# A fused attention and gMLP kernel: VectorE's exponential becomes one fourth power plus a linear term

## The chip, the core and the metric

The kernel runs on one core of a Trainium2 chip. The metric is the device time of one execution in microseconds; lower is better. The time before is the median of three runs.

## The reference

Two branches read the same input x (1 x 2048 x 512, bfloat16) and are mixed by a sigmoid gate per row. Branch A is attention with 32 heads of 16 channels that share one key and one value head. Branch B is a gMLP with a spatial matrix of 2048 x 2048.

```python
g = _sigmoid((x * gate_w).sum(-1, keepdims=True))
# A: H = 32, Dh = 16, one K and one V for all heads
q = (x @ wq).reshape(B, S, H, Dh).transpose(0, 2, 1, 3)
k = x @ wk
v = x @ wv
p = _softmax(jnp.einsum('bhqd,bkd->bhqk', q, k) * Dh ** (-0.5), axis=-1)
a = jnp.einsum('bhqk,bkd->bhqd', p, v).transpose(...).reshape(B, S, H * Dh) @ wo
# B: Fh = 688
z = _gelu(jnp.einsum('bsd,df->bsf', x, w_in))
z1 = z[..., :Fh]; z2 = _layernorm(z[..., Fh:])
gg = jnp.einsum('ts,bsf->btf', w_sp, z2) + b_sp[None, :, None]
b = jnp.einsum('bsf,fd->bsd', z1 * gg, w_out)
out = g * a + (1 - g) * b
```

## The kernel before

**Blocks.** The scores of all heads are 32 x 2048 x 2048 numbers. The kernel cuts them into 32 units. A unit is four heads and 512 queries, and within it there are 16 key tiles of 128 keys for each of the four heads (called groups, g). One block is 128 keys by 512 queries of one head, so a unit has 64 blocks and the kernel 2048. TensorE (PE) computes a block with a 32-row matmul (`s_mm`) into one of the eight PSUM banks; four such matmuls, one for each group, can run side by side. The exponential of a block is a 128 x 512 tile in SBUF, and a second matmul (`o_mm`) multiplies it by the 128 x 32 tile of V (with a column of ones for the softmax's sum) and adds it up in bank 6, four groups side by side again. Four matmuls side by side are called a round here.

**Two ways to an exponential.** ScalarE (ACT) reads two or three banks with one `Exp` and writes bfloat16 into a ring of `PB` = 16 tiles called P (`exp_op`, line 827). VectorE (DVE) makes a part of the blocks by a polynomial in float16. A batch is one key tile of a unit, four blocks (2048 columns). For a batch, `d_A` (line 839) reads the score s from PSUM and writes Q_A * s + Q_AS into a buffer U; `d_u` (line 846) squares U in place; `d_w` (line 852) squares once more, out of place, into a buffer W. The exponential is approximated, up to a common factor, by W's fourth power, the second power in U with a weight, a linear term and a constant. So each block has two products with V: U meets V1, and W meets VW, a copy of V scaled by Q_CW that GpSimd (POOL) makes at the start (line 570). The linear and the constant term need no elementwise work: per unit they are one matmul each with sums over the keys that are formed once (KTV and SVB). There are `ND` = 5 pairs of U and W.

`d_w` is shared: VectorE or POOL does it, in pieces of 256 columns, eight to a batch. POOL works upward from the end of a batch and VectorE from its start.

**The gMLP and the rest.** PE's other work comes in small pieces that fill the time between the blocks: the projections, z1 and z2 (win times x), the spatial product (`g_sp`), the outputs (`g_out`). After z1 and z2 are there, at some 160 us, ACT breaks off its exponentials for one stretch of GELU (`gelu_ops`, line 653), with a change of its function table on either side. VectorE then takes the statistics of z2 (line 659), POOL raises the variance to the power of -0.5 (line 668), and VectorE normalises z2 (line 673).

**The planner.** The order of all instructions on all engines is fixed before the kernel runs, by a planner written in Python in the same file: it plays through the run with estimated durations for PE, ACT, VectorE and POOL (`pe_step`, `act_step`, `dve_step`, `pool_step`) and issues, at each step, what its rules choose. Semaphores follow from the reads and writes of tiles (`Prog.op`). Its rules have numbers that were chosen by hand or search, in `PR`. These matter here:

- VectorE has two banks of its own, `DBK` = (5, 4). The second is shared with ACT's three-bank steps; `FLEX` says up to which backlog of VectorE it goes to VectorE instead.
- `D_HG` is the backlog of VectorE below which PE refills its banks right after a score step.
- POOL starts a piece of `d_w` only where VectorE's next work reads PSUM for long enough (`psum_work`, `pool_try`), since the planner takes VectorE's SBUF squares and POOL's to exclude each other (`lock`).
- `WRES` is the reserve of pieces that VectorE leaves to POOL when it is not urgent; pieces of the unit that PE is adding up come first (`poly_step`).
- `NXT` and `RMIN` bound how far VectorE works ahead into the next unit and how late in a unit a batch may start.
- When PE has nothing, it runs filling matmuls with zeros as long as its busy share over the last 3400 ns is under `W_MIN`.

A batch's buffer is free again when all its products with V have been issued (`dleft`). A flag computed on the chip compares the largest |q|^2 |k|^2 with 0.985 * Q_B^2; where it is exceeded, all of attention is computed again in a general way.

Of the kernel before, what the change touches and what calls it, by code (L numbers as in the profile page):

```python
# [7 lines left out]
ALU = mybir.AluOpType  # L8
# [7 lines left out]
D = 512  # L16
# [7 lines left out]
PB = 16  # L24
ND = 5
NQ = 3
NMAX = 8
NXT = 32
Q_B = 0.74
Q_A = 0.4770697274170593  # L30
Q_AS = 0.5048945666981567
Q_C0 = 0.6939921791513274
Q_C1 = 0.32473621688265525
Q_CW = 0.78515625
# [13 lines left out]
A_OV = 63.7  # L48
# [5 lines left out]
C_P0 = 184.0  # L54
C_WT = 4500.0
# [5 lines left out]
PR = dict(HALF=50.0, IDR=10, IDN=4, WRES=20, D_HG=2400.0, D_FL=False, WIN=1000.0, WIH=560.0, BACK=30, PRESS=5, FLEX=3000.0, RMIN=32, WBL=0.4, W_MIN=0.85, TTR=0.0, PMX=3, WMX=1000.0, PTO=6000.0, PSL=80.0, WP0=45000.0, WG=0, HOLD=0.0, RLEND=0)  # L61
# [109 lines left out]
def build_kernel(nc, x_d, wq_d, wk_d, wv_d, wo_d, win_d, wsp_d, bsp_d, wout_d, gw_d, out_d):  # L171
    es = ExitStack()
    with es:
# [13 lines left out]
        def bkey(b):  # L187
            return ("bk", b)
# [11 lines left out]
        VW = sb("VW", [128, NMAX, 32], B16)  # L200
# [6 lines left out]
        UW = sb("UW", [128, 2, ND, 2048], F16)  # L207
# [35 lines left out]
        wq_raw = UW[:, 1, ND - 1, :].bitcast(B16).rearrange("p (a n) -> p a n", a=4)  # L243
# [297 lines left out]
        def g_V(c, b=BM):  # L541
            nw = 2 * DH + 1
            kn = 4 * c + 4 > NKT - NMAX

            def piece(k, dt):
                t0 = 512 * c + 128 * k
                return lambda: fm(b, nw, 64 * k, xT[:, dt, t0:t0 + 128], wvg[:, dt, 0:nw], dt == 0, dt == 3, ["wv", "gw", "wvk", ("x", c)], "V")
            src = bank(b, 256).rearrange("p (k w) -> p k w", w=64)
            evs = []

            def e1():
                op("dve", lambda v: v.tensor_copy(V1[:, 4 * c:4 * c + 4, 0:DH], src[:, :, 0:DH]), r=[bkey(b)], w=[("V", c)], tag="Vev")

            def e2():
                op("dve", lambda v: v.tensor_scalar(gs[:, 4 * c:4 * c + 4].unsqueeze(2), src[:, :, 2 * DH:2 * DH + 1], E_MAX, None, ALU.min), r=[bkey(b)], w=[("gs", c)], tag="gsev")

            def e3(e):
                k0 = 4 * c - (NKT - NMAX)
                return lambda: op("dve", lambda v: v.tensor_scalar(KN[:, k0:k0 + 4, e, 16 * e:16 * e + 16], src[:, :, DH:2 * DH], 0.25, None, ALU.mult),  # L559
                                  r=[bkey(b)], w=["KN"], tag="KNev")  # L560
            evs = [(150.0, e1), (100.0, e2)]
            if kn:
                evs += [(140.0, e3(0)), (140.0, e3(1))]

            def done(t):
                T[("V", c)] = t
                if kn:
                    k0 = 4 * c - (NKT - NMAX)
                    fin = kn and all(("V", c2) in T for c2 in (2, 3))
                    dq(pl_q, 600.0, lambda: op("pool", lambda g: g.tensor_scalar(VW[:, k0:k0 + 4, :], V1[:, 4 * c:4 * c + 4, :], Q_CW, None, ALU.mult),  # L570
                                               r=[("V", c)], w=["VW"], tag="VW"), t, setT("VW") if fin else None)
# [77 lines left out]
        def gelu_ops():  # L649
            out = []  # L650
            for k in range(4):
                def f(k=k):
                    op("act", lambda a: a.activation(z2[:, 4 * k * FH:4 * (k + 1) * FH], z2[:, 4 * k * FH:4 * (k + 1) * FH], ACT.Gelu_apprx_tanh),  # L653
                       r=[("z2", 4 * k + i) for i in range(4)], w=[("z2", 4 * k + i) for i in range(4)], tag="gelu2")
                    t = clk["now"] + 2600.0
# [9 lines left out]
                    if k == 3:  # L665
                        def pw():
                            op("dve", lambda v: v.tensor_scalar(ve[:], mv[:, :, 1], LN_EPS, None, ALU.add), r=[("mv", i) for i in range(NST)], w=["ve"])
                            op("pool", lambda g: g.tensor_tensor(rstd[:], ve[:], nhalf[:], ALU.pow), r=["ve", "nhalf"], w=["rstd"])
                            t2 = clk["now"] + 4500.0
                            zc = [NST]  # L670
                            for st in range(NST):
                                def zn(st=st):
                                    op("pool" if st in ZP else "dve", lambda v: v.tensor_scalar(z2[:, FH * st:FH * st + FH], z2[:, FH * st:FH * st + FH], mv[:, st, 0:1],  # L673
                                                                        rstd[:, st:st + 1], ALU.subtract, ALU.mult),
                                       r=[("mv", st), "rstd", ("z2", st)], w=[("z2", st)], tag="z2n")
                                    zc[0] -= 1
                                    if not zc[0]:
                                        T["z2n"] = clk["now"] + (C_ZN if st in ZP else 370.0) + 200.0
                                if st in ZP:
                                    dq(pl_q, C_ZN, zn, t2, None)  # L680
                                else:
                                    dq(dve_q, 370.0, zn, t2, "tt")
                        dq(dve_q, 220.0, pw, t)
                out.append((2490.0, f, []))
            for ft in range((NZ - ZD) // 4):
                def f(ft=ft):
                    op("act", lambda a: a.activation(z1[:, ft, :], z1[:, ft, :], ACT.Gelu_apprx_tanh), r=[("z1", ft)], w=[("z1", ft)], tag="gelu1")
                    T[("gelu", ft)] = clk["now"] + 2000.0
                out.append((1905.0, f, [("z1", ft, tc) for tc in range(4)]))
# [147 lines left out]
        def d_A(m, i, b, n=1):  # L837
            s = m % ND
            op("dve", lambda v: v.tensor_scalar(UW[:, 0, s, 512 * i:512 * (i + n)], bank(b, 512 * n), Q_A, Q_AS, ALU.mult, ALU.add),  # L839
               r=[bkey(b + j) for j in range(n)], w=[("U", s, h) for h in range(i, i + n)], tag="dA")  # L840

        def d_u(m, h0, h1):
            s = m % ND
            src = UW[:, 0, s, 1024 * h0:1024 * h1]
            k = [("U", s, h) for h in range(2 * h0, 2 * h1)]
            op("dve", lambda v: v.tensor_tensor(src, src, src, ALU.mult), r=k, w=k, tag="dTT")  # L846

        def d_w(eng, m, a, b, after=()):
            s = m % ND
            src = UW[:, 0, s, 256 * a:256 * b]  # L850
            w = [("W", s, i) for i in range(a, b)] + (["wqr0", "wqr1"] if s == ND - 1 else [])
            op(eng, lambda v: v.tensor_tensor(UW[:, 1, s, 256 * a:256 * b], src, src, ALU.mult),  # L852
               r=[("U", s, h) for h in range(a // 2, (b + 1) // 2)], w=w, after=after, tag="dTT" if eng == "dve" else "pTT")
# [146 lines left out]
        gst = {"on": False, "arm": False, "t": 0.0}  # L1000
# [51 lines left out]
        def new_batch(now):  # L1052
# [6 lines left out]
            for u in (ua, ua + 1):  # L1059
# [24 lines left out]
                dleft[m] = 8  # L1084
# [448 lines left out]
        def act_step(now):  # L1533
# [12 lines left out]
            if gst["arm"] and (gel or dz["i"] < NZ or dz["cur"] is not None or dz["full"]) and st_["ke"] == st_["kf"] or gst["on"]:  # L1546
                r = None
                extra = 0.0 if gst["on"] else 1300.0
# [45 lines left out]
        def uw_add(m, z, a, b, t):  # L1594
            u, kt, gl = batches[m]
            s = m % ND
            lw = V1[:, kt, :] if z == 0 else VW[:, kt - (NKT - NMAX), :]
            lk = ("V", kt // 4) if z == 0 else "VW"
            if z:
                wh = whalf[m]  # L1600
                for i in range(a, b):
                    wh[i] = t
                rng = [i for i in range(a // 2, (b + 1) // 2) if 2 * i in wh and 2 * i + 1 in wh]
            else:
                rng = range(a, b)
            for i in rng:
                g = gl[i]
                if z:
                    t = max(wh[2 * i], wh[2 * i + 1])
                add_item(u, g, (t, lambda last, u=u, g=g, i=i: o_mm(  # L1610
                    u, g, lw, UW[:, z, s, 512 * i:512 * i + 512], [lk, ("W", s, 2 * i), ("W", s, 2 * i + 1)] if z else [lk, ("U", s, i)], last), lk, ("D", m)))

# [9 lines left out]
        def poly_step(now, only, full=False, idle=False):  # L1622
            av = sum(w_avail(m, now) for m in pq)
            for m in sorted(pq):
# [3 lines left out]
                if ud < hd // 2 and th <= now and not (full and hd // 2 - ud < 2 and ud == 0):  # L1628
# [3 lines left out]
                    uw_add(m, 0, 2 * ud, hd // 2 * 2, now + c_ + D_END + L_X)  # L1632
# [19 lines left out]
                uw_add(m, 1, wb, wb + n, now + c_ + D_END + L_X)  # L1652
# [26 lines left out]
        def pool_try(now, rem=0.0):  # L1679
# [7 lines left out]
            for x in pl_q:  # L1687
# [6 lines left out]
                plc["lock"] = now + x[0]  # L1694
# [11 lines left out]
            for m in sorted(pq):  # L1706
# [9 lines left out]
                uw_add(m, 1, i - n, i, now + c_ + 100.0 + L_X)  # L1716
# [115 lines left out]
        if INFO is not None and st_["pu"] < NU:  # L1832
            print(pv_done[st_["pu"]], unit_total(st_["pu"]), pv_g[st_["pu"]], [[(x[0], x[3]) for x in q] for q in pv_items[st_["pu"]]], clk, {k: T.get(k) for k in ("KTV", "SVB", "VW", ("QS", 0))})
# [177 lines left out]
```

## Time and profile before

| | |
|---|---|
| median of 3 runs | 727.26 us (726.29 to 727.68) |
| the profiled execution | 727.22 us, of which the span from the first to the last instruction is 725.4 us |
| granted PE clock, mean | 0.998 |
| blocks made by ACT | 1480 (matmuls of P with V) |
| blocks made by VectorE | 568 (matmuls of U with V, and as many of W with VW) |
| DMA | 20.12 MB, mean 28 GB/s |

In the profile PE is the matmul row, PEld the weight load, and lines are those of the kernel's source. A group row gives line, engine, operation, what is written and read, the shapes (partitions x elements), the count, then after the bar the busy time in us and the mean duration of one in ns, and after the second bar the engine's idle time just before and what ended it. All matmuls have line 388, so they are told apart by names: `ps<-QA,KA` are scores, `ps<-P,V` the products of ACT's exponentials, `ps<-UW,V` and `ps<-UW,VW` those of VectorE's. A row of the waits gives the total in us, the times and the longest. A row of the timeline gives start and duration in us, then engine, line and count, with the idle time before it in brackets. A row of the windows gives the stretch in us, its length, then busy time of PE, PEld, DVE, ACT and POOL with counts, the granted clock, the DMA share and GB/s. Where one tile is asked for, a row gives the count, minimum, median and maximum in ns, first and last start, and the shapes.

### The profile page before, as it was taken

The numbers are of one execution on the slowest core, as the hardware profiler recorded it, in microseconds if no ns is written. First come the engines' busy times: TensorE is split into PE (matmuls) and PEld (weight loads), VectorE is DVE, ScalarE is ACT, GpSimd is POOL, SyncE is SP. The second block draws the span as 40 slices with busy tenths as digits, with TensorE's granted clock in tenths as the row PEclk, the third lists the DMA queues.
The fourth block names the chain that finished last, engine by engine and source line by source line (L and its number), as shares of the span: only waits on it lengthen the run. The fifth ranks groups of instructions, "written<-read, shape, count | busy, mean of one in ns | idle before, by whom it ended". The sixth has DMA issues, their size and how long they took to land.

```text
span 725.4 us, 21992 instructions
## 1 busy us (share of the span) xinstructions
PE 706.7 (97%) x9052; PEld 207.7 (29%) x9052; DVE 702.9 (97%) x1061; ACT 705.8 (97%) x748; POOL 519.4 (72%) x491
## 2 busy tenths in 40 slices
PE   8999999999899999999999999999999999999997
PEld 3332333224222222222222222222223222222222
DVE  4999999999999999999999999999999999999996
ACT  5999999999999999999999999999999999999995
POOL 5558787685767777777686766777777777787761
PEclk9999999999999999999999999999999999999999
DMA  9442000000002003200001041000003300000101
GB/s 161 130 101 60 2 3 2 2 1 3 1 2 31 3 1 74 60 15 2 2 1 38 2 106 36 9 2 1 2 2 82 73 17 9 2 2 2 31 2 34
DMA packets 59810, 20.12 MB, mean 28 GB/s; under 512 B 54804, under 2 KB 59192, under 8 KB 59704
## 3 DMA queue, kind: packets, MB, share of 16 engines
q1 hardware_dynamic: 57448, 18.36, 11.8%
q8 instruction: 73, 1.20, 0.7%
q10 hardware_dynamic: 2256, 0.30, 0.3%
q14 instruction: 33, 0.27, 0.1%
HBM read 3.38 MB, written 2.10 MB: 8 GB/s over the span
## 4 chain that ended last, share of the span: by engine, by line
PE 63%; DVE 22%; ACT 9%; issue 5%; DMA 1%; POOL 0%; ACTq 0%; DVEq 0%; POOLq 0%
PE ps L388 63%; DVE UW L839 10%; ACT P L827 8%; DVE UW L846 4%; DVE UW L852 2%; DVE bst L659 2%; DMA xT<-in_A_x_dram 1%; DVE T L864 1%; DVE z L711 0%; DVE QA L531 0%; POOL UW L852 0%; ACT z L653 0%; DVE z L673 0%; DVE z L645 0%; DVE km L513 0%
## 5 line engine op out<-in xcount | busy, mean ns | idle before, releaser
L827 ACT ACTIVATE P<-ps 128x1024 bf16<-128x1024 f32 (+1 forms) x728 | 680.3, 1140 | 3.7 <-PE ps L388 3.0
L852 POOL TENSOR_TENSOR UW<-UW 128x512 f16<-128x512 f16 (+2 forms) x351 | 423.1, 1205 | 147.2 <-DVE UW L852 52.9
L839 DVE TENSOR_SCALAR UW<-ps 128x512 f16<-128x512 f32 (+1 forms) x449 | 357.1, 817 | 4.1 <-PE ps L388 3.9
L388 PE MATMUL ps<-QA,KA 32*128 32x512 bf16 x2048 | 308.1, 384 | 10.2 <-DVE UW L839 4.9
L388 PE MATMUL ps<-P,V 128*32 128x512 bf16 x1480 | 211.1, 385 | 0.2 <-DVE KN L559 0.2
L846 DVE TENSOR_TENSOR UW<-UW 128x2048 f16<-128x2048 f16 (+1 forms) x189 | 182.1, 966 | 1.3
L388 PEld LDWEIGHTS ps<-QA,KA 32*128 32x128 bf16 x2048 | 81.4, 91 | 305.9 <-ACT P L827 141.7
L388 PE MATMUL ps<-UW,VW 128*32 128x512 f16 x568 | 126.4, 384 | 0.2 <-DVE UW L852 0.2
L388 PE MATMUL ps<-wT,z 128*32 128x512 bf16 (+1 forms) x1536 | 118.3, 366 | 0.0
L852 DVE TENSOR_TENSOR UW<-UW 128x1024 f16<-128x1024 f16 (+3 forms) x164 | 98.2, 609 | 1.1 <-POOL UW L852 0.8
L388 PE MATMUL ps<-UW,V 128*32 128x512 f16 x568 | 88.1, 384 | 0.8 <-DVE T L864 0.5
L388 PEld LDWEIGHTS ps<-P,V 128*32 128x32 bf16 x1480 | 48.9, 94 | 51.8 <-issue 48.0
L388 PEld LDWEIGHTS ps<-wT,z 128*32 128x32 bf16 x1536 | 29.6, 94 | 43.2 <-issue 41.8
L388 PEld LDWEIGHTS ps<-UW,VW 128*32 128x32 bf16 x568 | 30.0, 94 | 17.9 <-issue 13.1
L535 POOL TENSOR_TENSOR QSQ<-QA 128x512 bf16<-128x512 bf16 x16 | 24.2, 1511 | 14.0 <-DVE UW L852 6.1
L388 PE MATMUL ps<-wout,z 128*32 128x512 bf16 x384 | 31.5, 384 | 0.0
L388 PE MATMUL ps<-win,xT 128*32 128x344 bf16 x512 | 29.9, 312 | 0.1
L388 PEld LDWEIGHTS ps<-UW,V 128*32 128x32 bf16 x568 | 21.0, 94 | 19.1 <-issue 12.9
L864 DVE STREAM_TRANSPOSE T<-ps 128x512 f32<-128x512 f32 (+1 forms) x33 | 22.6, 687 | 2.2 <-PE ps L388 2.2
L388 PE MATMUL ps<-CT,SVB 128*32 128x512 bf16 x128 | 24.1, 383 | 0.0
L388 PE MATMUL ps<-QA,KTV 128*32 128x512 bf16 x128 | 23.3, 383 | 0.0
L388 PE MATMUL ps<-xT,win 128*32 128x512 bf16 (+1 forms) x384 | 22.7, 363 | 0.2 <-ACT P L827 0.2
(116 smaller groups left out, 364.9 us busy)
## 6 DMA issues: line engine op xcount, KB each, us to landing
out_dram<-outsb SPq DMA_DIRECT2D x15, 128.0 KB, 1.7
win<-in_B_w_in_dram SPq DMA_DIRECT2D x1, 1376.0 KB, 7.9
wout<-in_B_w_out_dram SPq DMA_DIRECT2D x1, 640.0 KB, 4.2
wo<-in_A_wo_dram SPq DMA_DIRECT2D x8, 64.0 KB, 2.3
KA<-KA SPq DMA_DIRECT2D x4, 112.0 KB, 2.9
UW<-in_A_wq_dram SPq DMA_DIRECT2D x1, 384.0 KB, 4.2
wT<-in_B_w_sp_dram SPq DMA_TRANSPOSE x16, 4.5
UW<-in_A_wq_dram ACTq DMA_DIRECT2D x1, 128.0 KB, 4.2
```

What stands on the lines that cost most here:

```text
L388: return t.matmul(dst, lhsT, rhs, start=start, stop=stop, tile_position=tp)
L535: dq(pl_q, 1050.0, lambda: op("pool", lambda v: v.tensor_tensor(QSQ[:, q % 2, :], QA[:, q % NQ, :], QA[:, q % NQ, :], ALU.mult), r=[("Q", ...
L659: dq(dve_q, 410.0, lambda st=st, h=h: op("dve", lambda v: v.bn_stats(bst[:, st, h, :], z2[:, FH * st + 344 * h:FH * st + 344 * h + 344]), ...
L827: op("act", lambda a: a.activation(P[:, 512 * p0:512 * (p0 + n)], ps[:, 512 * b0:512 * (b0 + n)], ACT.Exp), r=[bkey(b0 + i_) for i_ in ran ...
L839: op("dve", lambda v: v.tensor_scalar(UW[:, 0, s, 512 * i:512 * (i + n)], bank(b, 512 * n), Q_A, Q_AS, ALU.mult, ALU.add), r=[bkey(b + j) ...
L846: op("dve", lambda v: v.tensor_tensor(src, src, src, ALU.mult), r=k, w=k, tag="dTT")
L852: op(eng, lambda v: v.tensor_tensor(UW[:, 1, s, 256 * a:256 * b], src, src, ALU.mult), r=[("U", s, h) for h in range(a // 2, (b + 1) // 2) ...
L864: return lambda: pgx.op("dve", lambda v: v.transpose(T1[:, jj, c0:c1], bank(BO, c1 - c0, c0)), r=[bkey(BO)], w=[("T1", jj, c0)], tag="T1")
```

## The change

The polynomial becomes (Q_A * s + Q_AS)^4 plus a linear term and a constant, with new coefficients and a narrower bound (Q_B from 0.74 to 0.68). U no longer meets V, only the second squares do, with V1 itself; VW and its two POOL instructions are gone. `d_w` squares in place, so a batch has one buffer, of which there are six (`ND`). The P ring has 24 tiles. A batch has four products with V instead of eight.

In the planner, the power on POOL becomes an entry at the head of POOL's queue with a duration of 3440 ns, and the normalisation is queued when it has been issued; the GELU instructions that follow the change of the table are 1300 ns later (`gst["x"]`). Several numbers of `PR`, and NXT (32 to 24) and A_OV, are different.

```diff
-PB = 16
-ND = 5
+PB = 24
+ND = 6
-NXT = 32
-Q_B = 0.74
+NXT = 24
+Q_B = 0.68
...
-PR = dict(HALF=50.0, ..., WRES=20, D_HG=2400.0, ..., BACK=30, PRESS=5, FLEX=3000.0, RMIN=32, WBL=0.4, W_MIN=0.85, ...)
+PR = dict(HALF=100.0, ..., WRES=16, D_HG=2800.0, ..., BACK=32, PRESS=5, FLEX=5000.0, RMIN=36, WBL=0.5, W_MIN=0.8, ...)
...
-        UW = sb("UW", [128, 2, ND, 2048], F16)
+        UW = sb("UW", [128, ND, 2048], F16)
...
-                    t = clk["now"] + 2600.0
+                    t = clk["now"] + 2600.0 + gst["x"]
...
-                            op("pool", lambda g: g.tensor_tensor(rstd[:], ve[:], nhalf[:], ALU.pow), r=["ve", "nhalf"], w=["rstd"])
-                            t2 = clk["now"] + 4500.0
+                            t2 = clk["now"] + 250.0
+                            pl_q.appendleft((C_POW, lambda: op("pool", lambda g: g.tensor_tensor(rstd[:], ve[:], nhalf[:], ALU.pow), r=["ve", "nhalf"], w=["rstd"]),
+                                             lambda: t2 if clk["now"] < t2 else -1e9, zns))
...
         def d_w(eng, m, a, b, after=()):
             s = m % ND
-            src = UW[:, 0, s, 256 * a:256 * b]
-            op(eng, lambda v: v.tensor_tensor(UW[:, 1, s, 256 * a:256 * b], src, src, ALU.mult),
+            src = UW[:, s, 256 * a:256 * b]
+            op(eng, lambda v: v.tensor_tensor(src, src, src, ALU.mult),
...
-                dleft[m] = 8
+                dleft[m] = 4
...
-            return (64 - 4 * n) + 8 * n + (8 if n else 0) + (4 if chk_of(u) is not None else 0)
+            return 64 + (8 if n else 0) + (4 if chk_of(u) is not None else 0)
...
-                    uw_add(m, 0, 2 * ud, hd // 2 * 2, now + c_ + D_END + L_X)
...
-                uw_add(m, 1, wb, wb + n, now + c_ + D_END + L_X)
+                w_add(m, wb, wb + n, now + c_ + D_END + L_X)
```

`w_add` adds a block's one product with V1 once both of its 256-column pieces have their second square.

More of the change, by code (lines that the diff above doesn't have):

```diff
@@ L47 @@
 N0 = 3
-A_OV = 63.7
+A_OV = 63.3
 HEAD = 45000.0
@@ L54 @@
 C_P0 = 184.0
+C_POW = 3440.0
 C_WT = 4500.0
@@ L60 @@
 W_GEL = 0.98
-PR = dict(HALF=50.0, IDR=10, IDN=4, WRES=20, D_HG=2400.0, D_FL=False, WIN=1000.0, WIH=560.0, BACK=30, PRESS=5, FLEX=3000.0, RMIN=32, WBL=0.4, W_MIN=0.85, TTR=0.0, PMX=3, WMX=1000.0, PTO=6000.0, PSL=80.0, WP0=45000.0, WG=0, HOLD=0.0, RLEND=0)
+PR = dict(HALF=100.0, IDR=10, IDN=4, WRES=16, D_HG=2800.0, D_FL=False, WIN=1000.0, WIH=560.0, BACK=32, PRESS=5, FLEX=5000.0, RMIN=36, WBL=0.5, W_MIN=0.8, TTR=0.0, PMX=3, WMX=1000.0, PTO=6000.0, PSL=80.0, WP0=45000.0, WG=0, HOLD=0.0, RLEND=0)
 SCHED = {}
@@ L665, in f, with zn @@
                     if k == 3:
+                        zc = [NST]
+                        def zn(st):
+                            op("dve", lambda v: v.tensor_scalar(z2[:, FH * st:FH * st + FH], z2[:, FH * st:FH * st + FH], mv[:, st, 0:1],
+                                                                rstd[:, st:st + 1], ALU.subtract, ALU.mult),
+                               r=[("mv", st), "rstd", ("z2", st)], w=[("z2", st)], tag="z2n")
+                            zc[0] -= 1
+                            if not zc[0]:
+                                T["z2n"] = clk["now"] + 570.0
@@ L670, in pw @@
[L670 to L682, printed above, removed]
+                            t2 = clk["now"] + 250.0
@@ L838, in d_A @@
             s = m % ND
-            op("dve", lambda v: v.tensor_scalar(UW[:, 0, s, 512 * i:512 * (i + n)], bank(b, 512 * n), Q_A, Q_AS, ALU.mult, ALU.add),
-               r=[bkey(b + j) for j in range(n)], w=[("U", s, h) for h in range(i, i + n)], tag="dA")
+            op("dve", lambda v: v.tensor_scalar(UW[:, s, 512 * i:512 * (i + n)], bank(b, 512 * n), Q_A, Q_AS, ALU.mult, ALU.add),
+               r=[bkey(b + j) for j in range(n)],
+               w=[("U", s, h) for h in range(i, i + n)] + [("W", s, h) for h in range(2 * i, 2 * i + 2 * n)] + (["wqr0", "wqr1"] if s == ND - 1 else []), tag="dA")
         def d_u(m, h0, h1):
             s = m % ND
-            src = UW[:, 0, s, 1024 * h0:1024 * h1]
+            src = UW[:, s, 1024 * h0:1024 * h1]
             k = [("U", s, h) for h in range(2 * h0, 2 * h1)]
@@ L1592, in w_avail, with w_add @@
             return min(4 * ud, 8 - pw) - wb if tu <= now else 0
-        def uw_add(m, z, a, b, t):
+        def w_add(m, a, b, t):
             u, kt, gl = batches[m]
             s = m % ND
[L1597 to L1611, printed above, removed]
+            wh = whalf[m]
+            for i in range(a, b):
+                wh[i] = t
+            for i in range(a // 2, (b + 1) // 2):
+                if 2 * i in wh and 2 * i + 1 in wh:
+                    g = gl[i]
+                    add_item(u, g, (max(wh[2 * i], wh[2 * i + 1]), lambda last, u=u, g=g, i=i: o_mm(
+                        u, g, V1[:, kt, :], UW[:, s, 512 * i:512 * i + 512], [("V", kt // 4), ("W", s, 2 * i), ("W", s, 2 * i + 1)], last), ("V", kt // 4), ("D", m)))
         def w_end(m):
@@ L1693, in pool_try @@
                 x[1]()
-                plc["lock"] = now + x[0]
+                if x[0] != C_POW:
+                    plc["lock"] = now + x[0]
                 plc["free"] = now + x[0] + 60.0
```

30 lines of the change are left out of this document (14 added, 16 removed).

## The prediction

> **What bounds the kernel now.** I read the page from the top: busy shares and clock, then the chain of waits, then the costliest groups.
>
> ```profile
> span 725.4 us, 21992 instructions
> PE 706.7 (97%) x9052; PEld 207.7 (29%) x9052; DVE 702.9 (97%) x1061; ACT 705.8 (97%) x748; POOL 519.4 (72%) x491
> PEclk9999999999999999999999999999999999999999
> PE 63%; DVE 22%; ACT 9%; issue 5%; DMA 1%; POOL 0%; ACTq 0%; DVEq 0%; POOLq 0%
> ```
>
> Three engines stand at 97%, and the chain names PE. To tell which of them really sets the end I take the groups and the waits.
>
> ```profile
> L827 ACT ACTIVATE P<-ps 128x1024 bf16<-128x1024 f32 (+1 forms) x728 | 680.3, 1140 | 3.7 <-PE ps L388 3.0
> L852 POOL TENSOR_TENSOR UW<-UW 128x512 f16<-128x512 f16 (+2 forms) x351 | 423.1, 1205 | 147.2 <-DVE UW L852 52.9
> L839 DVE TENSOR_SCALAR UW<-ps 128x512 f16<-128x512 f32 (+1 forms) x449 | 357.1, 817 | 4.1 <-PE ps L388 3.9
> L388 PE MATMUL ps<-P,V 128*32 128x512 bf16 x1480 | 211.1, 385 | 0.2 <-DVE KN L559 0.2
> L846 DVE TENSOR_TENSOR UW<-UW 128x2048 f16<-128x2048 f16 (+1 forms) x189 | 182.1, 966 | 1.3
> L388 PE MATMUL ps<-UW,VW 128*32 128x512 f16 x568 | 126.4, 384 | 0.2 <-DVE UW L852 0.2
> L852 DVE TENSOR_TENSOR UW<-UW 128x1024 f16<-128x1024 f16 (+3 forms) x164 | 98.2, 609 | 1.1 <-POOL UW L852 0.8
> L388 PE MATMUL ps<-UW,V 128*32 128x512 f16 x568 | 88.1, 384 | 0.8 <-DVE T L864 0.5
> PEld ps L388 <- ACT P L827: 142.2, 341, 1.2
> PEld ps L388 <- DVE UW L839: 96.7, 232, 2.1
> ```
>
> The exponentials of ACT lose 3.7 us to waiting in the whole run, and VectorE's PSUM reads (the line in d_A) 4.1 us. PE's weight loads, however, sit 142.2 us waiting for an exponential to free its bank and 96.7 us for a PSUM read. So PE, busy or not, is mostly the one that waits: the chain runs through it because every score goes through it. The bound is the common capacity of ACT and VectorE. They share 2048 score blocks of 128x512: ACT 1480, VectorE 568, which is 142 batches of four.
>
> From this an exchange rate follows, and all gains below go through it. A block on ACT costs 680.3 / 1480 = 0.460 us, a batch 1.839. A batch on VectorE costs (357.1 + 182.1 + 98.2) / 142 = 4.489 us. If s us of VectorE come free, the planner can move s / (4.489 + 1.839) batches over, and the end moves by 1.839 / 6.328 = **0.291 s**. One us freed on ACT moves it by 4.489 / 6.328 = **0.709 us**.
>
> **The change part by part.**
>
> First squares no longer meet V. 568 matmuls go, four to a round.
>
> ```profile
> 717.26 1.47 PE L388 MATMUL ps<-wout,z 128*32 128x512 bf16 x24
> ```
>
> Six back-to-back rounds end after 1.47 us where one matmul lasts 0.384: (1.47 - 0.38) / 5 = 0.218 us a round. So 142 rounds are 31.0 us of PE. Off the bound, this is worth only the waits it shortens. These are the ones that PE relief can reach:
>
> ```profile
> 170.47 1.45 ACT L1411 ACTIVATE z<-ps 128x1536 bf16<-128x1536 f32 x1 [1.12 <-PE ps L388]
> 15.86 1.23 DVE L839 TENSOR_SCALAR UW<-ps 128x1024 f16<-128x1024 f32 x1 [1.90 <-PE ps L388]
> 717.27 0.78 DVE L864 STREAM_TRANSPOSE T<-ps 128x256 f32<-128x256 f32 x2 [1.53 <-PE ps L388]
> 715.97 0.38 PE L388 MATMUL ps<-UW,V 128*32 128x512 f16 x1
> ```
>
> The 1.90 at 15.86 is the start, before any square has met V, and stays. Of VectorE's remaining 2.0 us of waits for PE, and of ACT's 1.12 in the GELU stretch, I take half: 1.0 x 0.291 + 0.56 x 0.709 = 0.7 us. At the end VectorE waits 1.53 us for the last accumulation, in which first squares still ran at 715.97; one round of them there is 0.2 us. Together **-0.9**; ends 0 and -2.
>
> The planner's gMLP durations. The GELU times now include the table load (1300 ns), the power on POOL is a queued operation of 3440 ns, and the normalisation is queued when it has been issued.
>
> ```profile
> 164.97 1.77 DVE L659 BATCH_NORM_STATS2 bst<-z 128x6 f32<-128x344 bf16 x4 [1.53 <-ACT z L653]
> 184.54 3.44 POOL L668 TENSOR_TENSOR rstd<-ve,nhalf 128x16 f32<-128x16 f32 x1
> 188.15 2.96 POOL L852 TENSOR_TENSOR UW<-UW 128x512 f16<-128x512 f16 x3 [0.17 <-PE ps L388]
> 188.09 2.46 DVE L673 TENSOR_SCALAR z<-z,mv,rstd 128x688 bf16<-128x688 bf16 x2
> 191.08 0.81 DVE L673 TENSOR_SCALAR z<-z,mv,rstd 128x688 bf16<-128x688 bf16 x2
> 191.70 10.55 ACT L827 ACTIVATE P<-ps 128x1024 bf16<-128x1024 f32 x10 [1.40 <-PE ps L388]
> ```
>
> Now the statistics are placed too early and VectorE stands 1.53 us. POOL squares planned beside PSUM reads are stuck behind the power until 188.15, fall on the normalisation, and two of its instructions take 2.46 instead of 0.81 us; the bank reads behind it come late, PE stands behind them, and ACT misses 1.40 us at 191.70. Placed with the right durations these go: (1.53 + 1.65) x 0.291 + 1.40 x 0.709 = **-1.9**. If something else is late next there (the z pieces on PE), half; ends 0 and -1.9. What queues behind the power on POOL is the squares; they wait as now, but the planner no longer counts on them.
>
> Squares in place and six buffers instead of five pairs. Work per batch is the same: one PSUM read, two squares. In place or not costs VectorE the same, by the first square (in place today) and the second (not):
>
> ```profile
> L846 DVE TENSOR_TENSOR UW<-UW 128x1024 f16<-128x1024 f16 x94 | 64.8, 691 | 0.4
> L852 DVE TENSOR_TENSOR UW<-UW 128x1024 f16<-128x1024 f16 x96 | 64.7, 680 | 0.1
> L852 POOL TENSOR_TENSOR UW<-UW 128x512 f16<-128x512 f16 x169 | 244.9, 1449 | 90.4 <-DVE UW L852 42.2 <-DVE UW L839 22.8 <-PE ps L388 6.8
> L852 POOL TENSOR_TENSOR UW<-UW 128x256 f16<-128x256 f16 x151 | 118.7, 786 | 43.6 <-DVE UW L839 15.1 <-DVE UW L852 6.8 <-DVE UW L846 5.4
> L852 POOL TENSOR_TENSOR UW<-UW 128x768 f16<-128x768 f16 x31 | 59.5, 1919 | 13.3 <-DVE UW L839 4.2 <-DVE UW L852 4.0 <-DVE UW L846 3.0
> ```
>
> POOL in place is not in this trace; from 691 to 680 I bound it at 2% of 423.1 us either way, 8.5 us or 12 pieces of 256 columns by its own price, and take 0 (ends -0.6 and +0.6).
>
> What can matter is who does the second square. In pieces of 256 columns POOL does 2 x 169 + 151 + 3 x 31 = 582 of 1136, and VectorE 554 for 98.2 us, 0.177 us each. POOL only takes a piece while VectorE reads PSUM, so it does more when both VectorE banks are refilled at once, which a freer PE and the larger D_HG (2400 to 2800) and FLEX (3000 to 5000) favour. The nearest stretch is the one from 660 to 711 us, where little of the gMLP is left for PE:
>
> ```profile
> L839 DVE TENSOR_SCALAR UW<-ps x27: 676/1158/1224, 660.9 to 708.9; 128x1024 f16<-128x1024 f32 x14, 128x512 f16<-128x512 f32 x13
> L852 POOL TENSOR_TENSOR UW<-UW x30: 612/998/2350, 659.9 to 710.9; 128x256 f16<-128x256 f16 x16, 128x512 f16<-128x512 f16 x11, 128x768 f16<-128x768 f16 x3
> ```
>
> Half of its PSUM reads come in pairs, and POOL does 16 + 22 + 9 = 47 of 82 pieces, 57% against 51% overall. I take half of that difference, 54% or 31 pieces: 31 x 0.177 x 0.291 = **-1.6**. Ends: POOL loses a tenth of its 582 (WRES falls from 20 to 16, which lets VectorE take squares sooner): +3.0; POOL takes half of VectorE's 554: 277 x 0.177 x 0.291 = -14.3.
>
> The rest. The two VW instructions ran on POOL before 22 us, when no second square goes there yet: 0. The deeper P ring: the exponentials' whole waiting is 3.7 us, 3.0 of it for PE, so no room for a gain: 0. The load of wq lies in the last buffer, first needed one batch later: 0. RMIN, NXT, BACK, HALF, WBL and W_MIN shift where batches and filling fall, not what a batch costs; I take 0 and let the ends of the squares' split cover them. Three-bank exponentials become rarer still:
>
> ```profile
> L570 POOL TENSOR_SCALAR VW<-V 128x128 bf16<-128x128 bf16 x2 | 1.1, 534 | 0.3 <-DVE UW L839 0.2
> ...
> L827 ACT ACTIVATE P<-ps 128x1536 bf16<-128x1536 f32 x25 | 38.9, 1556 | 0.9 <-PE ps L388 0.9
> L827 ACT ACTIVATE P<-ps 128x1024 bf16<-128x1024 f32 x702 | 650.9, 1126 | 2.8 <-PE ps L388 2.1
> ```
>
> A block costs 0.519 us in the former and 0.464 in the latter, so nothing is lost by it: 0, end +0.6.
>
> Sum: -0.9 - 1.9 - 1.6 = -4.4 us. The profiled execution took 727.22 us (span 725.4 and 1.8 around it), as good as the median of 727.26; so **722.8 us**.
>
> **The rivals.**
>
> *PE was the brake* (713 us). The chain's 63% speak for it, and 31 us of PE is 4%. It would work only by handing VectorE more: ACT is full, so the end can come forward only if squares leave VectorE. With half of VectorE's second squares on POOL it is -14.3. Against: POOL already stands 147.2 us before its squares for VectorE's sake and is busy 72%. The Trainium skill, "Perfetto Trace Analysis", section Identifying the Most-Contended Engine, says matmul occupancy is a bad measure and weight-load busy time a better one; by that rule PE, at 29%, is not the bound, and the waits above agree.
>
> *Hidden anyway* (727). The gMLP stalls come back elsewhere and POOL's share stays: what is left is the first part's 0.9 or less, 726.3 to 727.2. For it speaks that ACT and VectorE have so little waiting to lose.
>
> *Slower: VectorE takes squares back* (730). All four products of a batch now exist only after the second square, where half could enter the accumulation after the first; a unit's end and its buffers hang on POOL's last piece. The planner lets VectorE finish the squares of the unit that PE is accumulating before any bank read, and WRES is smaller. Each piece that so moves costs 0.177 x 0.291 = 0.05 us. The 2.8 us of the first two parts are eaten from 54 pieces on; 110 pieces, a fifth of POOL's, give +3.0 net, and so do 58 where those gains did not come. Against it: POOL waits for VectorE today, not the other way (0.8 us in all).
>
> *Slower: the clock.* PE falls by 31 us, and its filling matmuls now keep 80% busy instead of 85.
>
> ```profile
> L387 PE MATMUL ps<-CT 128*128 128x512 bf16 x11 | 4.8, 620 | 1.4 <-DVE CT L262 1.4
> 180.00:200.00 20.00, 17.46 (x278) 6.48 (x270) 19.87 (x41) 18.48 (x18) 13.91 (x14) 1.00 0.01 2
> ```
>
> The first matmuls of the run take 620 ns instead of 384; the least busy stretch later, 17.46 of 20 us, kept the full clock. If matmuls ran at 620 for some 10 us, PE would lose 10 x (1 - 384 / 620) = 3.8 us, and if ACT lost as much: +2.7, 730. The Trainium skill, "TensorE: Matmul & The Clock Gate", Part 1, has the clock halved after an idle window of about 3.4 us; by that rule 80% filling keeps it, and the stretch above agrees.
>
> *The slow path.* The kernel recomputes all if |q||k| passes a bound, now 0.985 x 0.68^2 = 0.455 instead of 0.539. From the reference's inputs I work out 2.936 x 0.1366 = 0.401 for the largest squares: it stays off.
>
> **How the numbers follow.** Measurement can tell about 0.2%, 1.45 us. Chances: the forecast (719 to 725.8) 0.50; PE the brake (below 719) 0.16; hidden 0.15; VectorE takes squares back 0.15; clock 0.02; everything else that is slower 0.02. Faster 0.66, same 0.15, slower 0.19. The low end takes in the brake's price, 713; the high end a tenth of POOL's pieces lost with none of the gains, 730.3. About 1 in 10 lies outside on each side.
>
> **What would show it.** Groups with VW are gone and UW,V matmuls equal four times the batches; 143 to 145 batches, so P,V matmuls near 1470. Second squares on VectorE below 95 us and POOL above 582 pieces. No wait of bst on ACT, no double-length normalisation, no 1.4 us hole in ACT after the GELU stretch. PE's busy time hardly lower, since waits and filling replace the rounds. The prediction is wrong if POOL's share falls, if batches stay at 142 or below, or if they rise above 147.

## The result and the profile after

The changed kernel takes 723.19 us (723.15 to 723.93), before it was 727.26; the ratio is 0.9947, with a 95% interval of 0.9936 to 0.9959. The prediction was 722.8. The profiled execution took 723.15 us with a span of 721.3, 4.1 us less than before. The time came out as forecast; the way there did not in all parts.

These are the page's busy line and the groups that answer to those shown of before (line 825 is the exponential, 837 `d_A`, 845 the first square, 851 the second), then the paired reads and POOL's squares by shape.

```profile
PE 700.9 (97%) x8572; PEld 204.6 (28%) x8572; DVE 702.4 (97%) x1014; ACT 704.6 (98%) x759; POOL 519.7 (72%) x469
L825 ACT ACTIVATE P<-ps 128x1024 bf16<-128x1024 f32 (+1 forms) x739 | 679.4, 1211 | 1.8 <-PE ps L387 1.5
L837 DVE TENSOR_SCALAR UW<-ps 128x512 f16<-128x512 f32 (+1 forms) x418 | 356.4, 874 | 3.2 <-PE ps L387 1.8
L387 PE MATMUL ps<-P,V 128*32 128x512 bf16 x1480 | 186.9, 386 | 0.2 <-DVE KN L558 0.2
L845 DVE TENSOR_TENSOR UW<-UW 128x2048 f16<-128x2048 f16 (+1 forms) x176 | 182.3, 1036 | 1.3
L387 PE MATMUL ps<-UW,V 128*32 128x512 f16 x568 | 109.6, 385 | 0.2
L851 DVE TENSOR_TENSOR UW<-UW 128x1024 f16<-128x1024 f16 (+5 forms) x161 | 99.4, 629 | 0.0
L387 PE MATMUL ps<-CT,zer 128*32 128x512 bf16 x256 | 23.2, 382 | 0.0
L837 DVE TENSOR_SCALAR UW<-ps 128x1024 f16<-128x1024 f32 x150 | 182.2, 1215 | 2.1 <-PE ps L387 1.7
L851 POOL TENSOR_TENSOR UW<-UW 128x512 f16<-128x512 f16 x165 | 247.9, 1502 | 84.2 <-DVE UW L851 39.8 <-DVE UW L837 25.4 <-DVE z L641 4.6
L851 POOL TENSOR_TENSOR UW<-UW 128x256 f16<-128x256 f16 x129 | 103.9, 805 | 38.6 <-DVE UW L851 15.5 <-DVE UW L837 9.4 <-DVE UW L845 1.2
L851 POOL TENSOR_TENSOR UW<-UW 128x768 f16<-128x768 f16 x37 | 74.9, 2024 | 21.1 <-DVE UW L845 8.2 <-DVE UW L837 6.4 <-DVE UW L851 4.4
```

568 products are gone from PE, filling matmuls rose from 168 to 256, and PE is still 97% busy. The split of the blocks did not move: ACT 1480, VectorE 568, 142 batches. VectorE's three groups cost 638.1 us (637.4 before). POOL did 2 x 165 + 129 + 3 x 37 = 570 pieces (582 before). So nothing went from one engine to the other; both only wait less.

Where the 4.1 us went is read from ACT, which is never idle for long from its first exponential to its last. Five rows of its timeline cut the run (start, duration): the first exponentials, the two loads of the function table around the GELU stretch, the next exponentials, and the last ones. First before, then after.

```profile
9.16 18.94 ACT L827 ACTIVATE P<-ps 128x1536 bf16<-128x1536 f32 x19 [0.89 <-PE ps L388]
161.14 1.28 ACT L653 ACT_TABLE_LOAD   x1
183.90 1.28 ACT L827 ACT_TABLE_LOAD   x1
185.19 5.12 ACT L827 ACTIVATE P<-ps 128x1024 bf16<-128x1024 f32 x5
696.91 19.46 ACT L827 ACTIVATE P<-ps 128x1024 bf16<-128x1024 f32 x20
```

```profile
9.01 18.54 ACT L825 ACTIVATE P<-ps 128x1536 bf16<-128x1536 f32 x19 [0.89 <-PE ps L387]
155.25 1.28 ACT L649 ACT_TABLE_LOAD   x1
176.85 1.28 ACT L825 ACT_TABLE_LOAD   x1
178.15 24.86 ACT L825 ACTIVATE P<-ps 128x1024 bf16<-128x1024 f32 x27
689.60 22.59 ACT L825 ACTIVATE P<-ps 128x1024 bf16<-128x1024 f32 x24
```

The stretch from the first table load to the next exponential fell from 24.05 to 22.90 us. The two stretches of exponentials fell from 151.98 + 531.18 to 146.24 + 534.04 us, by 2.9: 1.4 of that is the hole behind the GELU stretch, which is gone (178.15 runs on for 27 exponentials), and 1.5 is spread. The start is 0.15 earlier. After the last exponential 9.03 us were left, now 9.1. In sum -1.15 - 2.9 - 0.15 + 0.1 = -4.1.

The starts in the trace say what the 2.9 is made of. From its start to the start of the next, a two-bank exponential mostly takes 0.904 us and a three-bank one 1.33, before and after (0.452 and 0.443 us a block). What the stretches last beyond that sum is lateness, with a few other short instructions: 14.7 us before and 11.2 after. So 3.5 us of lateness went, 1.4 of them the hole, and the rarer three-bank exponentials (25 before, 3 after) cost 0.6.

The same cuts for the runs below; "exponentials" is brought to 1480 blocks with 1.84 us a batch:

| kernel | batches | median us | GELU stretch | exponentials | after the last |
|---|---|---|---|---|---|
| before | 142 | 727.26 | 24.1 | 683.2 | 9.0 |
| after | 142 | 723.19 | 22.9 | 680.3 | 9.1 |
| e4, durations | 141 | 725.47 | 22.8 | 679.4 | 10.4 |
| e6, polynomial | 141 | 727.17 | 24.5 | 680.7 | 9.2 |
| e7, polynomial, durations | 141 | 725.66 | 22.9 | 680.9 | 9.1 |
| e8, durations, numbers | 141 | 727.29 | 22.6 | 682.2 | 9.8 |
| e5, polynomial, numbers | 141 | 728.53 | 23.7 | 683.0 | 9.4 |

### The profile page after: what moved, and what is told of

Same layout as the page of the kernel before. It is cut to its first block, busy times and chain, and to the rows that moved or that the text cites. A ratio compares the mean times of both kernels' runs of the same rounds, so it can differ in the third digit from the quotient of the medians.

```text
span 721.3 us, 20958 instructions
## 1 busy us (share of the span) xinstructions
PE 700.9 (97%) x8572; PEld 204.6 (28%) x8572; DVE 702.4 (97%) x1014; ACT 704.6 (98%) x759; POOL 519.7 (72%) x469
## 5 line engine op out<-in xcount | busy, mean ns | idle before, releaser
L825 ACT ACTIVATE P<-ps 128x1024 bf16<-128x1024 f32 (+1 forms) x739 | 679.4, 1211 | 1.8 <-PE ps L387 1.5
L387 PE MATMUL ps<-QA,KA 32*128 32x512 bf16 x2048 | 322.1, 384 | 11.6 <-ACT P L825 6.8
L387 PE MATMUL ps<-P,V 128*32 128x512 bf16 x1480 | 186.9, 386 | 0.2 <-DVE KN L558 0.2
L387 PEld LDWEIGHTS ps<-QA,KA 32*128 32x128 bf16 x2048 | 88.8, 91 | 312.5 <-ACT P L825 162.9
L387 PE MATMUL ps<-wT,z 128*32 128x512 bf16 (+1 forms) x1536 | 113.4, 366 | 0.0
L387 PE MATMUL ps<-UW,V 128*32 128x512 f16 x568 | 109.6, 385 | 0.2
L851 DVE TENSOR_TENSOR UW<-UW 128x1024 f16<-128x1024 f16 (+5 forms) x161 | 99.4, 629 | 0.0
L387 PEld LDWEIGHTS ps<-P,V 128*32 128x32 bf16 x1480 | 42.6, 94 | 59.9 <-issue 57.6
L387 PEld LDWEIGHTS ps<-UW,V 128*32 128x32 bf16 x568 | 25.4, 94 | 20.0 <-issue 14.8
L863 DVE STREAM_TRANSPOSE T<-ps 128x512 f32<-128x512 f32 (+1 forms) x33 | 22.8, 694 | 2.1 <-PE ps L387 2.1
L387 PE MATMUL ps<-CT,zer 128*32 128x512 bf16 x256 | 23.2, 382 | 0.0
L387 PE MATMUL ps<-CT,SVB 128*32 128x512 bf16 x128 | 22.8, 383 | 0.0
L387 PE MATMUL ps<-xT,wqd 128*32 128x512 bf16 x256 | 21.1, 384 | 0.3 <-DMA xT<-in_A_x_dram 0.2
```

Source lines behind the costliest of these rows:

```text
L387: return t.matmul(dst, lhsT, rhs, start=start, stop=stop, tile_position=tp)
L825: op("act", lambda a: a.activation(P[:, 512 * p0:512 * (p0 + n)], ps[:, 512 * b0:512 * (b0 + n)], ACT.Exp), r=[bkey(b0 + i_) for i_ in ran ...
L851: op(eng, lambda v: v.tensor_tensor(src, src, src, ALU.mult), r=[("U", s, h) for h in range(a // 2, (b + 1) // 2)], w=w, after=after, tag= ...
L863: return lambda: pgx.op("dve", lambda v: v.transpose(T1[:, jj, c0:c1], bank(BO, c1 - c0, c0)), r=[bkey(BO)], w=[("T1", jj, c0)], tag="T1")
```

## The experiments

Three theories were put up. A: the gain is waits taken away, above all in the GELU stretch. B: PE was the brake, and its relief is the gain. C: it is another draw of a planner that arranges 22000 instructions anew after any edit. First come three edits that keep the planned order of the instructions.

**e1: PE relief alone, in the old order.**

```diff
-                add_item(u, g, (t, lambda last, u=u, g=g, i=i: o_mm(
+                add_item(u, g, (t, lambda last, u=u, g=g, i=i: None if z == 0 and not last else o_mm(
```

> The kernel before in its own order, with the 568 products of the first squares with V left out (the output lacks the second-power term). It is PE relief alone, 31 us of it, with nothing planned anew. Theory A (PE is off the bound; the change gained by taking waits away, most of them in the GELU stretch): 0 to 1.5 us faster, 725.8 to 727.3, since ACT's exponentials wait 3.7 us in all. Theory B (PE was the brake): 3 us faster or more, 724 or below. Theory C (the gain is only another draw of the planner): no change, 727.3.

Measured 727.70 us (ratio 1.0006, 0.9993 to 1.0019): no change. ACT's row hardly moves:

```profile
L827 ACT ACTIVATE P<-ps 128x1024 bf16<-128x1024 f32 (+1 forms) x728 | 680.1, 1147 | 3.5 <-PE ps L388 2.9
```

3.5 us of waiting where it was 3.7. The trace counts what PE was really spared. If starts of products with V less than 0.1 us apart are taken as one round, before has 730 rounds, e1 646 and the change 578. Many of the products left out in e1 had shared a round with others, so it spares 84 rounds, 18 us at 0.218 us each, and not 31; the change itself spares 152, 33 us. Taking 18 us off PE is worth nothing by itself. Theory B in its simple form is out as far as that reaches; e6 below goes further.

**e2: a product with zeros ahead of each of VectorE's products, in the new order.**

```diff
+                    def f(last, u=u, g=g, i=i):
+                        o_mm(u, g, zer[:, 0:32], UW[:, s, 512 * i:512 * i + 512], ["zer", ...], False)
+                        o_mm(u, g, V1[:, kt, :], UW[:, s, 512 * i:512 * i + 512], [...], last)
```

> The changed kernel in its own order, with one more matmul of zero weights ahead of each of VectorE's 568 products: PE's load of before put back, the planner not told. Theory A: 0 to 1.5 us slower, up to 724.7. Theory B: 3 us slower or more, 726 or above. Theory C: no change.

Measured 746.20 us (ratio to before 1.0258, 1.0245 to 1.0272): 23.0 us slower than the change, which only B's "3 us slower or more" takes in. The groups of this run, and a piece of its timeline:

```profile
L387 PE MATMUL ps<-UW,zer 128*32 128x512 f16 x568 | 113.1, 385 | 0.1
L825 ACT ACTIVATE P<-ps 128x1024 bf16<-128x1024 f32 (+1 forms) x739 | 693.7, 1058 | 10.1 <-PE ps L387 3.9
L837 DVE TENSOR_SCALAR UW<-ps 128x512 f16<-128x512 f32 (+1 forms) x418 | 357.9, 872 | 17.0 <-PE ps L387 13.6
```

```profile
310.61 0.41 PE L387 MATMUL ps<-UW,zer 128*32 128x512 f16 x4
310.84 0.40 PE L387 MATMUL ps<-UW,V 128*32 128x512 f16 x4
311.06 0.38 PE L387 MATMUL ps<-UW,zer 128*32 128x512 f16 x1
311.06 0.38 PE L387 MATMUL ps<-P,V 128*32 128x512 bf16 x1
311.07 0.39 PE L387 MATMUL ps<-UW,zer 128*32 128x512 f16 x2
311.27 0.40 PE L387 MATMUL ps<-UW,V 128*32 128x512 f16 x3
```

VectorE now waits 17.0 us before its PSUM reads: PE has become the brake. But the edit does more than put the old load back. The product behind a zero matmul has the same group and comes a round later (310.61, 310.84), so a round that mixes both engines' products (311.06) becomes two. By the count of e1 this run has 838 rounds, 260 more than the change (57 us at 0.218) and 108 more than before. So e2 shows that the new order cannot bear 260 rounds more; that it could not bear the 152 of before is not shown.

ACT's waiting shows less as idle time (10.1 us) than in the mean duration of an exponential, 1211 ns after the change and 1058 here, while the stretch from 178 to 712 us grew to 552.7 us. An exponential that is issued early overlaps the one ahead, and its record is longer: two-bank exponentials that start after the one ahead has ended have a median of 1023 ns in all three traces, and there are 102 of them in e2, 15 before and 7 after the change. Before, the mean was 1140.

**e3: the power made cheap, in the old order.** POOL's power is replaced by a multiplication.

```diff
-op("pool", lambda g: g.tensor_tensor(rstd[:], ve[:], nhalf[:], ALU.pow)
+op("pool", lambda g: g.tensor_tensor(rstd[:], ve[:], nhalf[:], ALU.mult)
```

> The kernel before in its own order, with the power on POOL (3.44 us) replaced by a multiplication of the same 128x16 operands (the layer norm's scale is wrong). It takes away what POOL's squares stand behind. Theory A: the hole of 1.40 us in ACT after the GELU stretch and the double-length normalisation go, 1.4 us faster, 725.9. Theories B and C: no change beyond 0.5 us.

Measured 725.65 us (0.9974, 0.9964 to 0.9985), 1.7 us faster; A had said 1.4. Its timeline at the place of the hole:

```profile
184.13 0.72 POOL L668 TENSOR_TENSOR rstd<-ve,nhalf 128x16 f32<-128x16 f32 x1
187.68 0.82 DVE L673 TENSOR_SCALAR z<-z,mv,rstd 128x688 bf16<-128x688 bf16 x2
184.78 18.31 ACT L827 ACTIVATE P<-ps 128x1024 bf16<-128x1024 f32 x18
```

The normalisation takes 0.82 us for two where it took 2.46, and ACT runs on without a hole. The chain of the prediction (power, POOL's squares behind it, normalisation, bank reads, PE, ACT) is shown for the old order by taking away its head.

**e4 to e8: the change in its parts, planned anew.** Three parts: the gMLP durations, the polynomial with its rings, the numbers of the planner (PR, NXT, A_OV). e4 is before with the first, e6 with the second, e7 with both, e8 with the first and third, e5 with the second and third. The edits are those of the change; the durations also leave the power out of the planner's `lock`. The planner found 141 batches for all five, one less than before and the change have.

> The kernel before with the gMLP durations of the change alone (table load, power on POOL's queue), planned anew; two products with V, old numbers. The order that comes out has 141 batches on VectorE, one less than before, which by the exchange rate is 1.84 us more on ACT. Theory A: the 1.40 hole and about 1.15 us of the GELU stretch go, against 1.84: 0.7 us faster, 726.5. Theory B: no gain, 1.8 us slower by the batch, 729. Theory C: anything within 2 us either way.

> The kernel before with the new polynomial and its rings alone (one product with V, in place, six buffers, P ring of 24), old durations and old numbers of the planner, planned anew; 141 batches. Theory A: the stalls of the GELU stretch stay; 0 to 1 us faster, 726.3 to 727.3. Theory B: 2.3 us faster, 725.0. Theory C: within 2 us either way.

> The change with the planner's numbers of before (PR, NXT, A_OV), planned anew; 141 batches. Theory A: near all of the gain, 723.5 to 724.5. Theory B: the same. Theory C: the numbers were chosen for this program, so without them 1.84 us (a batch) or more is lost, 725 or above.

> The kernel before with the durations and the numbers of the change, but its old polynomial with two products with V, planned anew; 141 batches. Theory A: 725 to 725.5, as with the durations alone. Theory B: without PE relief the numbers bring nothing or cost, 725.5 or above. Theory C: within 2 us of 725.5 either way.

> The change without its gMLP durations (old GELU times, the power issued past POOL's queue), planned anew; 141 batches on VectorE. So far: before 727.3, with the durations alone 725.5, with all of the change 723.2. Theory A (the durations bring 1.8 us wherever they are applied, by taking the waits of the GELU stretch away): 725.0. Theory B (less work for PE lets the planner pack better; the durations matter little): 723.2 to 723.8. Theory C (a draw of the planner, one batch more or less is 1.84 us): 725.0 too, but with no stall in the GELU stretch.

Measured, where the kernel before took 727.2 to 727.3: e4 725.47 (0.997, 0.996 to 0.9981); e6 727.17 (0.9999, 0.999 to 1.0008); e7 725.66 (0.9976, 0.9967 to 0.9985); e8 727.29 (0.9997, 0.9988 to 1.0006); e5 728.53 (1.0016, 1.0007 to 1.0025).

The durations are worth 1.8 us on the old kernel and 1.5 with the new polynomial (e7 against e6). The polynomial is worth nothing alone (e6) and nothing beside the durations (e7 against e4). The numbers cost 1.8 us with the old polynomial (e8 against e4) and gain 2.5 with the new one (after against e7), of which 1.84 are the batch. So 1.5 to 1.8 us are theory A's, and the remaining 2.3 to 2.5 belong to the new polynomial and the numbers together. e6 is the wider test of relief, with 592 rounds where before has 730, and it gains nothing: its exponentials are 2.4 us better at equal blocks, and the missing batch (1.84) and a longer GELU stretch (0.4) take nearly all of that back. Of the forecasts for e4, e7 and e8, theory A's all missed by a microsecond or more; C's held.

The durations do not act by the same waits in every order. e6 has the old ones, and the wait of the statistics stays, but the hole is gone there too:

```profile
157.69 1.77 DVE L654 BATCH_NORM_STATS2 bst<-z 128x6 f32<-128x344 bf16 x4 [1.38 <-ACT z L648]
178.33 37.07 ACT L822 ACTIVATE P<-ps 128x1024 bf16<-128x1024 f32 x38
```

So the hole was a collision of the old order. What e7 has better than e6 is the GELU stretch, 22.9 us against 24.5.

The table says how these 2.3 us come about between e4 and the change: a batch more on VectorE, 1.84, and a shorter end, 1.3, against 0.9 that e4 has better in its exponentials. At the end of e4 PE is late. First e4 from its last product on, then the change:

```profile
713.28 1.68 PE L389 MATMUL ps<-wout,z 128*32 128x512 bf16 x24
714.59 1.24 PE L389 MATMUL ps<-wo,OT 128*32 128x512 bf16 x16
715.45 1.67 PE L389 MATMUL ps<-wout,z 128*32 128x512 bf16 x24
716.74 1.24 PE L389 MATMUL ps<-wo,OT 128*32 128x512 bf16 x16
718.67 1.41 DVE L760 SCALAR_TENSOR_TENSOR outsb<-ps,G,z 128x512 bf16<-128x512 f32 x2 [2.53 <-PE ps L389]
```

```profile
712.57 0.82 PE L387 MATMUL ps<-wout,z 128*32 128x512 bf16 x12
713.44 1.04 PE L387 MATMUL ps<-wo,OT 128*32 128x512 bf16 x14
715.40 1.41 DVE L755 SCALAR_TENSOR_TENSOR outsb<-ps,G,z 128x512 bf16<-128x512 f32 x2 [0.18 <-PE ps L387]
```

In e4 PE still has two whole output tiles to do, 80 matmuls, when the last exponential's product is in, and VectorE's final step waits 2.53 us for it; in the change PE is nearly done with them and the wait is 0.18. That this comes from the second product is not shown: the kernel before has two products as well, with 9.0 us after the last exponential and the same wait of 0.18, while e12 below has one product and 9.85 us.

e5 fell out of every forecast. Part of it is the clock. The windows of 5 us (busy PE, PEld, VectorE, ACT, POOL, then the granted clock) and a row of PE:

```profile
390.00:395.00 5.00, 4.76 (x38) 1.35 (x34) 5.00 (x10) 5.00 (x6) 4.23 (x4) 0.90 0.85 123
395.00:400.00 5.00, 5.00 (x44) 1.01 (x42) 3.41 (x5) 3.91 (x5) 2.83 (x4) 0.76 0.07 17
595.00:600.00 5.00, 5.00 (x47) 1.00 (x45) 3.79 (x7) 4.04 (x5) 2.96 (x5) 0.66 0.09 30
395.32 0.61 PE L386 MATMUL ps<-QA,KA 32*128 32x512 bf16 x3
```

The clock falls to 0.76, a score matmul takes 0.61 us instead of 0.38, and ACT stands for 1.1 us; at 595 us it happens again (clock 0.66, ACT busy 4.04 of 5). That is 2 us of e5's 5 against the change, a missing batch is 1.84, and up to 1.4 us lies outside the span (2.2 to 3.3 us there, 1.8 to 1.9 in the change). The executions agree: the two with a mean clock of 0.999 or more took 727.1 and 727.2 us, the four at 0.994 729.1 to 729.9.

**e9 to e12: numbers drawn anew for each polynomial.** To tell B from C, the planner's numbers were drawn by the same random walk for the old polynomial with the durations (e9, e10) and for the changed kernel (e11, e12), kept by the planner's own estimate.

```diff
 e9
-WRES=20, BACK=30, FLEX=3000.0, RMIN=32, W_MIN=0.85; NXT=32; RLAST=12
+WRES=24, BACK=32, FLEX=8000.0, RMIN=40, W_MIN=0.75; NXT=24; RLAST=8
 e10
-WRES=20, D_HG=2400.0, BACK=30, PRESS=5, FLEX=3000.0, RMIN=32, PSL=80.0; NXT=32
+WRES=16, D_HG=2000.0, BACK=24, PRESS=4, FLEX=8000.0, RMIN=36, PSL=160.0; NXT=28
 e11
-HALF=100.0, IDR=10, IDN=4, D_HG=2800.0, BACK=32, PRESS=5, FLEX=5000.0, RMIN=36, W_MIN=0.8, PSL=80.0; RLAST=12; W_GEL=0.98
+HALF=50.0, IDR=8, IDN=3, D_HG=3400.0, BACK=36, PRESS=3, FLEX=4000.0, RMIN=40, W_MIN=0.75, PSL=160.0; RLAST=8; W_GEL=0.95
 e12
-HALF=100.0, WRES=16, D_HG=2800.0, BACK=32, PRESS=5, FLEX=5000.0, RMIN=36, WBL=0.5, PSL=80.0; NXT=24; RLAST=12
+HALF=50.0, WRES=20, D_HG=2000.0, BACK=36, PRESS=8, FLEX=3000.0, RMIN=40, WBL=0.4, PSL=40.0; NXT=20; RLAST=8
```

> The kernel before with the change's gMLP durations, its old polynomial with two products with V, and numbers of the planner drawn anew for it (a random walk over PR, NXT, RLAST and W_GEL, kept by the planner's own estimate of the end); 142 batches. It asks whether the old polynomial with numbers of its own gets as far as the change. Theory B (PE relief is what lets the planner pack better): it stays above the change's 723.2, at 724.5 or above. Theory C (the numbers alone, drawn long enough, do it): 723 or below. Theory A says: the durations' 1.8 us and nothing more, 725.5.

> As the last, from a second random walk with other numbers; 142 batches. Theory A 725.5, theory B 724.5 or above, theory C 723 or below.

> The changed kernel with numbers of the planner drawn anew by the same random walk; 143 batches on VectorE, one more than the change. Theory B: PE relief leaves room, so new numbers still gain: a batch is 1.84 us, so 721.4. Theory C: no better than what the same walk finds for the old polynomial. A danger for all: W_MIN is 0.75 here, so PE may lose its clock for some us; then 723 to 725.

> The changed kernel with numbers from another walk (W_MIN 0.80, D_HG 2000, WRES 20, PRESS 8); 142 batches. Theory B: 721.5 to 723. Theory C: within 1 us of what the old polynomial gets.

Measured, where the kernel before took 727.47 us: e9 726.89 (0.9996, 0.9987 to 1.0005), e10 726.08 (0.9982, 0.9973 to 0.9991), e11 723.75 (0.9981, 0.9953 to 1.0009; seven of its twelve executions took 723.1 to 723.8, the other five, with a mean clock of 0.975 to 0.987, 727.1 to 732.9), e12 724.13 (0.9951, 0.9939 to 0.9964). With the durations in place, four orders of the old polynomial lie between 725.5 and 727.3 (e4, e8, e9, e10) and four of the new between 723.2 and 725.7 (after, e7, e11, e12). So the new polynomial is worth some 2 us (of the lead over e9 and e10 about 0.5 lies outside the span), but only through an order that is looked for with it. Four orders each support that; they do not settle its size. Nor do they say what in it is worth them: with the relief of PE came six buffers instead of five pairs, a P ring of 24 and products that all come after the second square, and no run parts these. Where B and C had a number, B's held for the old polynomial (724.5 or above); for the new one both missed. e11 has one batch more than the change and is no faster: with four blocks fewer on ACT its stretches of exponentials last 681.0 us, where the change has 680.3. None beats the change.

## Why the prediction was right, and where not

The bound was read rightly as far as the runs reach: ACT and VectorE full, PE off the path, since 18 us less of PE gain nothing (e1). That 31.0 us go from PE was right too, by the 152 rounds. The time of 722.8 against 723.19 is in good part luck: one of its three terms (POOL's share) did not happen, another came about partly by other waits, and lateness that it did not see made up for them.

*The gMLP durations, -1.9.* The chain behind the hole is shown by e3, and the part measures -1.8 (e4, with a batch less) and -1.5 (e7 against e6). But the hole also goes without the durations (e6, e5), and the shorter GELU stretch, which the durations bring in both, was not in the forecast. The waits named for it are gone: the next exponential follows the GELU stretch at once, and the statistics begin with no idle time ahead of them:

```profile
159.53 1.79 DVE L655 BATCH_NORM_STATS2 bst<-z 128x6 f32<-128x344 bf16 x4
```

*Shorter waits for PE, -0.9.* ACT's 1.12 us inside the GELU stretch is gone, but the durations alone shorten that stretch as far (22.8 in e4, 24.5 in e6 with the polynomial alone). That was put to the wrong part. VectorE's wait at the end fell from 1.53 to 0.71 us, more than the forecast's 0.2, yet the end is no shorter (9.0 and 9.1 us after the last exponential).

*POOL's share, -1.6.* This step failed. POOL was to go from 582 to about 613 pieces and did 570; VectorE's second squares cost 99.4 us instead of 98.2, and the batches stayed at 142. The prediction named both as signs that would make it wrong. The stretch from 660 to 711 us was a bad model: pairs did become more frequent, 150 of 418 PSUM reads against 119 of 449, and POOL took no more for it.

*The exchange rate.* No run tests it by itself; e11, where a batch did move, gained nothing. In the change none moved, so each us that ACT no longer waited came forward in full, not at 0.709: the hole and the GELU stretch are 2.55 us by themselves. Some 1.5 us more went out of the exponentials, and the prediction did not see them in 3.7 us of idle time: lateness is 14.7 us by the starts. Why it fell is open. The rarer three-bank exponentials are not it. The prediction read 0.519 us a block from them against 0.464, from durations that overlap; by the starts they are the cheaper ones, 0.443 against 0.452.

*The rivals.* PE as the brake got 0.16: wrong as put, since no square left VectorE and neither e1 nor e6 gains. The 2 us of the draws may yet be its relief, used by a new order; that is not shown. The clock got 0.02 as a cause of a loss: the change itself keeps it, yet e5, the same kernel without the durations, loses it twice.

## What to carry to other kernels

When an order is planned on estimated durations, correct the durations first: a wrong one (here 3.44 us on POOL that the plan did not count) shows as a hole on another engine, three releases further on. Relief on an engine off the bound was worth nothing here in the old order. Test it by leaving work out and by putting work in, and count in the trace what the edit did to the engine: 568 matmuls left out were 84 rounds, and 568 put in were 260. Cut the run on the fullest engine into a start, its stretches and an end: a few rows tell where the time went when no share of busy time moves.

## What was not expected of the hardware

The mean duration of an overlapped exponential tells of slack: 1058 ns where ACT waited for PE throughout, 1140 before, 1211 after, while one follows the other after some 0.92 us (534.04 us for 582 of two banks). It does not follow the time of the kernel: the two-bank ones have 1191 ns in e5, the slowest order, and 1138 in e12. The recorded idle time was 10.1, 3.7 and 1.8 us, far less than the difference in time; the lateness by the starts was 33.9, 14.7 and 11.2.

PE lost its clock with 80% filling planned: in e5 it ran at 0.90 and 0.76 in two windows of 5 us that show PE 4.76 and 5.00 us busy. The busy time of the first does not tell of it. The trace's record of the clock has it at half from 393.98 us for 3.41 us, and again from 595.37 us for 3.41. 80% alone does not bring it about: the change has the same W_MIN and a mean clock of 0.999 or more in each execution. The Trainium skill, "TensorE: Matmul & The Clock Gate", Part 1, has the clock at full or half and halves it after an idle window of about 3.4 us. The 0.23 us that a matmul takes longer (0.61 against 0.38) is about what one round takes at full clock, 0.218, so a halved rate agrees with the run; a PE idle for 3.4 us does not, by these rows.
